# Loading q and k four heads per transfer, 18 tokens to a partition, in an attention and mixer kernel

## The chip, the cores and the metric

The kernel runs on one core of a Trainium2 chip. The metric is the device time of one execution in microseconds (us), as the median of several runs. The engines are PE (TensorE, the matrix unit), DVE (VectorE), ACT (ScalarE), POOL (GpSimd) and SP (SyncE, which here issues most of the DMA transfers). PEld is the loading of PE's weights. The granted clock is the share of PE's full clock that the chip's throttle allowed, as the profile reports it. In lines of the profile, L823 is a line of the kernel's source (the same line is L824 in the changed kernel), and names such as pmx or uTa are the kernel's buffers. A quad below is the set of four heads (of eight) that the kernel loads and processes together.

## The reference

The shapes are batch 8, heads 8, sequence 576, head dimension 64. Causal attention with a position bias from a running sum is followed by a token mixer and a channel mixer:

```python
def _attn_ref(q, k, v, s):
    scores = scale * np.matmul(q, k.transpose(0, 1, 3, 2))
    cum = np.cumsum(np.maximum(s, 0.0), axis=-1)
    bias = -(cum[:, :, :, None] - cum[:, :, None, :])
    scores = np.where(causal, -1000000000.0, scores + np.minimum(bias, 0.0))
    # ... softmax over the last axis, then attn @ v

def _moe_ref(x, w_tok1, w_tok2, w_ch1, w_ch2):
    h = np.maximum(x.transpose(0, 2, 1) @ w_tok1, 0.0) @ w_tok2
    u = x + h.transpose(0, 2, 1)
    h2 = np.maximum(u @ w_ch1, 0.0) @ w_ch2
    return u + h2
```

q and k are drawn with a standard deviation of 0.1, so that q·k/8 is of the order of 0.01. The bias dominates the scores.

## The kernel before

The kernel holds a planner in Python. It collects operations with an estimated cost for each engine that may run them, simulates the engines, and emits the instructions in the order that the simulation gave. An operation with several alternatives (for instance an eviction on ACT or DVE) goes where the simulation has room. The program keeps this order: every engine is given its own fixed list. Where PE has nothing to do in the plan's first 95 us, the planner also puts filler products of zeros; they are presumably meant to keep PE's clock up.

The parts that the change touches are the load of q and k, and the block transposes that consume it:

```python
    R = 2
    # ... ring of four fp32 buffers of [128, 1152], ring of four bf16 ones
    def load_quad(src, b, qd):
        f = Buf(r_qf)
        for g in range(4):
            load_op(lambda g=g: nc.sync.dma_start(
                out=f.t[32 * g : 32 * g + 32, :].rearrange("p (k n) -> p k n", n=R * D),
                in_=src[b, 4 * qd + g, :, :].rearrange("(k p r) d -> p k (r d)", p=32, r=R)),
                [(f, g)], S / R * 0.027 / 16)
        return f
    # ... the quad is cast to bf16 (on POOL, except for batch 0), then
            P.op(dve(576, lambda n=n, dst=dst: nc.vector.transpose(
                out=dst.t[:, 0:S, :].rearrange("d t e -> d (t e)").bitcast(FP32).rearrange(
                    "d (k p r) -> d k r p", p=32, r=R),
                in_=n.t[:, :].bitcast(FP32))), ...)
```

Each head takes 32 partitions. With R = 2, a partition holds nine runs of two neighbouring tokens (512 bytes each in DRAM). DVE transposes blocks of 32×32 four-byte elements (pairs of bf16); the 32 values that a block writes to one partition belong to tokens two apart, so they lie 8 bytes apart. `dve(576, ...)` is the planner's estimate for a transpose: 0.67 us.

## Time and profile before

332.36 us is the median of 3 runs (332.08 to 334.28). The profiled run's span is 333.4 us.

The page's busy line of the kernel before gives each engine's busy time, its share of the span and its instructions:

```profile
PE 300.1 (90%) x2557; PEld 167.4 (50%) x2593; DVE 181.4 (54%) x404; ACT 168.6 (51%) x269; POOL 86.8 (26%) x110
```

PE is busy nine tenths of the time, but the groups by line add 29.4 us of filler, and the chain of waits (the work that ended last, followed back to what released it, as shares of the span by engine and by line) says that a large part of the span was not set by PE:

```profile
PE 42%; DMA 29%; SPq 11%; DVE 9%; issue 4%; POOL 2%; ACT 1%; POOLq 0%; ACTq 0%; DVEq 0%
PE pmx L823 19%; PE pmx L841 15%; DMA qkf<-in_q_dram 12%; SPq L535 7%; DMA qkf<-in_k_dram 6%; SPq L562 4%; DMA wc<-in_moe_w_ch_dram 3%; DMA vf<-in_v_dram 3%; PE pmx L749 3%; DMA w<-in_moe_w_tok_dram 3%; PE pav L682 3%; DVE E L652 2%; PE psc L628 2%; POOL qkn L581 1%; DVE ub L777 1%
```

DMA, and SP's queue that issues it, hold 40% of the chain. In order of time they are most of its first 134 us; after that it is mostly PE. The table of stretches shows the same. Its columns are the stretch in us from the span's start, its length, busy us and instructions of each engine, the granted PE clock, the DMA engines' busy share (over 1 where packets overlap) and GB/s:

```profile
core 0: us, PE busy (x) PEld busy (x) DVE busy (x) ACT busy (x) POOL busy (x), PEclk, DMA share, GB/s
0.00:40.00 40.00, 33.42 (x277) 18.18 (x281) 25.38 (x64) 16.62 (x19) 16.81 (x39) 0.91 1.17 193
40.00:90.00 50.00, 43.93 (x472) 27.59 (x479) 30.71 (x69) 28.28 (x46) 24.83 (x24) 0.98 1.15 217
90.00:140.00 50.00, 42.98 (x366) 24.46 (x368) 29.79 (x68) 28.97 (x48) 18.57 (x19) 0.89 1.12 199
140.00:230.00 90.00, 84.22 (x729) 44.83 (x739) 55.83 (x118) 55.93 (x88) 26.59 (x29) 1.00 0.83 172
230.00:310.00 80.00, 78.65 (x636) 43.74 (x643) 36.20 (x84) 35.03 (x62) 0.00 (x0) 1.00 0.24 63
```

Up to 140 us the DMA share is above 1.1 at some 200 GB/s. In 90 to 140 us PE has 7.0 us of idle time and a clock of 0.89. Most of that idle time is one wait. In the list of PE's waits (who waited for whom: us in total, times, longest us) it comes first:

```profile
PE pmx L823 <- DMA uTa<-ua: 6.5, 1, 6.5
```

uTa is filled by transposing DMAs that SP issues in order, behind loads of q and k that are themselves waiting. One more line says how fast q and k come in. It is a stretch in which almost nothing but q and k moved:

```profile
124.00:128.00 4.00, 3.65 (x38) 1.58 (x36) 3.10 (x7) 1.94 (x2) 0.00 (x0) 1.00 1.24 203
```

203 GB/s is typical of such stretches. The packet records of the trace have 46,080 packets of 512 bytes for q and k, 45 ns long in the median and 27 ns at the tenth percentile.

The transposes, by their source line, with minimum, median and maximum in ns:

```profile
L607 DVE STREAM_TRANSPOSE kT<-qkn x16: 760/776/780, 9.5 to 242.7; 128x576 f32<-128x576 f32 x16
L607 DVE STREAM_TRANSPOSE qT<-qkn x16: 729/770/781, 12.6 to 245.2; 128x576 f32<-128x576 f32 x16
```

### The profile page before, as it was taken

How to read it: one execution, taken by the hardware profiler on the slowest of the kernel's cores; microseconds unless marked ns; L12 is line 12 of the kernel's file. 1: busy time of each engine (PE TensorE's matmuls, PEld its weight loads, DVE VectorE, ACT ScalarE, POOL GpSimd, SP SyncE). 2: the span in 40 equal slices, each digit the busy share in tenths (PEclk: the TensorE clock that was granted, in tenths of full speed). 3: DMA queues.
4: the chain of work that ended last, by engine and by line, in shares of the span. 5: the costliest groups of instructions: out<-in, count | busy, mean ns of one | idle time of the engine just before them, and what ended most of it. 6: DMA issues, size and time to landing. Idle time of an engine off the chain costs nothing.

```text
span 333.4 us, 6640 instructions
## 1 busy us (share of the span) xinstructions
PE 300.1 (90%) x2557; PEld 167.4 (50%) x2593; DVE 181.4 (54%) x404; ACT 168.6 (51%) x269; POOL 86.8 (26%) x110
## 2 busy tenths in 40 slices
PE   6798999879799993899899998997999999999992
PEld 2356685435566441444466443543575445446640
DVE  4685642588678753116874583958561744350030
ACT  1364581347769455364397445973474418306500
POOL 3175225473737422051216120270000000000000
PEclk9599999999789999699999999999999999999997
DMA  8999999999999999898798279992400430042031
GB/s 153 202 195 208 208 215 203 183 251 223 227 208 187 203 202 186 209 227 195 152 246 163 58 176 233 180 176 73 102 2 0 90 134 2 34 95 79 3 96 69
DMA packets 109640, 50.45 MB, mean 151 GB/s; under 512 B 55904, under 2 KB 104416, under 8 KB 109600
## 3 DMA queue, kind: packets, MB, share of 16 engines
q1 hardware_dynamic: 106192, 46.17, 70.3%
q0 software_dynamic: 3408, 3.77, 6.7%
q8 instruction: 22, 0.36, 0.5%
q14 instruction: 18, 0.15, 0.2%
HBM read 40.71 MB, written 9.44 MB: 150 GB/s over the span
## 4 chain that ended last, share of the span: by engine, by line
PE 42%; DMA 29%; SPq 11%; DVE 9%; issue 4%; POOL 2%; ACT 1%; POOLq 0%; ACTq 0%; DVEq 0%
PE pmx L823 19%; PE pmx L841 15%; DMA qkf<-in_q_dram 12%; SPq L535 7%; DMA qkf<-in_k_dram 6%; SPq L562 4%; DMA wc<-in_moe_w_ch_dram 3%; DMA vf<-in_v_dram 3%; PE pmx L749 3%; DMA w<-in_moe_w_tok_dram 3%; PE pav L682 3%; DVE E L652 2%; PE psc L628 2%; POOL qkn L581 1%; DVE ub L777 1%
## 5 line engine op out<-in xcount | busy, mean ns | idle before, releaser
L823 PEld LDWEIGHTS <-wc 128*128 128x128 bf16 x624 | 59.6, 100 | 41.9 <-issue 12.1
L647 ACT ACTIVATE E<-psc 128x1024 bf16<-128x1024 f32 x64 | 62.1, 1020 | 31.1 <-PE psc L628 30.4
L823 PE MATMUL pmx<-uTb,wc 128*128 128x320 bf16 x384 | 58.1, 306 | 0.3 <-DMA uTb<-us 0.2
L581 POOL CAST qkn<-qkf 128x1152 bf16<-128x1152 f32 x29 | 34.1, 1183 | 87.4 <-DMA qkf<-in_k_dram 23.9
L841 PE MATMUL pmx<-wc,gb 128*128 128x512 bf16 x231 | 54.3, 379 | 0.4
L823 PE MATMUL pmx<-uTa,wc 128*128 128x512 bf16 (+1 forms) x236 | 46.4, 345 | 7.7 <-DMA uTa<-ua 6.5
L830 ACT ACTIVATE gb<-pmx 128x320 bf16<-128x320 f32 x74 | 32.1, 438 | 35.4 <-PE pmx L823 31.0
L544 POOL TENSOR_TENSOR vp<-vf,wT 128x512 bf16<-128x512 f32 (+1 forms) x35 | 37.0, 1078 | 35.8 <-PE pav L682 21.1
L841 PE MATMUL pmx<-wc,ga 128*128 128x512 bf16 x184 | 44.3, 379 | 0.9 <-issue 0.3
L569 ACT ACTIVATE junk<-qkn 128x1152 bf16<-128x1152 bf16 x24 | 27.9, 1162 | 24.1 <-POOL qkn L581 23.7
L652 DVE TENSOR_TENSOR E<-E,keep 128x512 bf16<-128x512 bf16 x64 | 32.5, 514 | 13.6 <-ACT E L647 13.4
L841 PEld LDWEIGHTS <-gb 128*128 128x128 bf16 x240 | 22.5, 98 | 25.2 <-issue 0.4
L682 PEld LDWEIGHTS <-E 128*128 128x128 bf16 x576 | 26.4, 98 | 15.5 <-DVE E L660 2.5
L830 ACT ACTIVATE ga<-pmx 128x512 bf16<-128x512 f32 (+1 forms) x43 | 22.0, 515 | 21.8 <-PE pmx L823 18.0
L694 DVE TENSOR_TENSOR x<-pav,rc 128x320 bf16<-128x320 f32 x60 | 29.4, 491 | 1.8
L682 PE MATMUL pav<-vp,E 128*128 128x65 bf16 x540 | 27.4, 195 | 3.2 <-DVE E L660 2.1
L927 PE MATMUL pmx<-zero 128*128 128x512 bf16 (+5 forms) x88 | 26.4, 431 | 2.7 <-DVE zero L424 1.2
L689 DVE RECIPROCAL rc<-pav 128x5 f32<-128x5 f32 x60 | 11.4, 189 | 30.2 <-PE pav L682 29.8
L841 PEld LDWEIGHTS <-ga 128*128 128x128 bf16 x192 | 17.6, 98 | 19.7 <-issue 1.1
L628 PE MATMUL psc<-qT,kT 32*128 32x256 bf16 (+2 forms) x640 | 23.8, 253 | 3.9 <-ACT E L647 3.2
L628 PEld LDWEIGHTS <-kT 32*128 32x128 bf16 x640 | 15.8, 93 | 16.1 <-issue 14.9
L852 DVE TENSOR_TENSOR of<-pmx,ua 128x512 f32<-128x512 f32 x16 | 10.9, 683 | 20.8 <-PE pmx L841 11.3
(81 smaller groups left out, 240.2 us busy)
## 6 DMA issues: line engine op xcount, KB each, us to landing
qkf<-in_k_dram SPq DMA_DIRECT2D x80, 144.0 KB, 4.8
qkf<-in_q_dram SPq DMA_DIRECT2D x80, 144.0 KB, 5.4
vf<-in_v_dram SPq DMA_DIRECT2D x32, 256.0 KB, 5.8
out_dram<-of SPq DMA_DIRECT2D x32, 256.0 KB, 2.5
wc<-in_moe_w_ch_dram POOLq DMA_DIRECT2D x8, 384.0 KB, 11.3
vf<-in_v_dram SPq DMA_DIRECT2D x8, 128.0 KB, 5.0
out_dram<-of SPq DMA_DIRECT2D x8, 128.0 KB, 2.4
w<-in_moe_w_tok_dram POOLq DMA_DIRECT2D x2, 256.0 KB, 8.8
```

The costliest lines, as they stand in the source:

```text
L544: eng.tensor_tensor(out=vp.t[p0 : p0 + n, c, :, 0:D], in0=vf.t[p0 : p0 + n, c, :, :], in1=wT[p0 : p0 + n, cw, b * H : b * H + H].unsqueeze ...
L569: P.op({"ACT": (1.2, 1.6, lambda: nc.scalar.activation(out=junk[:, :], in_=src.t[:, :], func=AF.Square, accum_out=sq[:, col : col + 1]))}, ...
L581: nc.gpsimd.tensor_copy(out=n.t[:, :], in_=f.t[:, :])
L628: nc.tensor.matmul(out=pss[g // 2].t[:, g % 2, c0 : c0 + z - a], lhsT=kT.t[rows, j0 : j0 + 128, e], rhs=qT.t[rows, a:z, e], start=(e == 0) ...
L647: nc.scalar.activation(out=E.t[:, :, gi * 512 : gi * 512 + 512], in_=ps.t[:, :, :], func=AF.Exp, scale=0.125)
L652: nc.vector.tensor_tensor(out=o, in0=o, in1=keep[:, :].unsqueeze(1).unsqueeze(1).to_broadcast([128, 2, 2, 128]), op=ALU.mult)
L682: nc.tensor.matmul(out=o[:, ic, 0 : D + 1], lhsT=E.t[:, hh, d0 : d0 + 128], rhs=vp.t[:, jc, h + hh, 0 : D + 1], start=(jc == j_lo), stop=( ...
L694: nc.vector.tensor_tensor(out=x.t[:, :, (h + hh) * D : (h + hh + 1) * D], in0=o[:, :, 0:D], in1=rc.t[:, :].unsqueeze(2).to_broadcast([128, ...
L823: nc.tensor.matmul(out=pm.t[:, 0 : e - a], lhsT=wc1[:, m, cc * 128 : cc * 128 + 128], rhs=uT.t[:, m, a:e], start=(m == 0), stop=(m == NMC ...
L830: lambda cc=cc, pm=pm, a=a, e=e: nc.scalar.activation(out=g.t[:, cc, a:e], in_=pm.t[:, 0 : e - a], func=AF.Relu),
L841: nc.tensor.matmul(out=pm.t[:, :], lhsT=g.t[:, cc, c * 128 : c * 128 + 128], rhs=wc2[:, cc, :], start=(cc == 0), stop=(cc == NCC - 1))
L927: f.fn = lambda t=r.tiles[slots[0]], n=n: nc.tensor.matmul(out=t[:, 0:n], lhsT=zero[:, 0:128], rhs=zero[:, 0:n], start=True, stop=True)
```

## The change

The intent is to load a whole quad in one transfer over 128 partitions, with 18 consecutive tokens (4,608 contiguous bytes) per partition. The price is that DVE's transposes write every 18th token, which is a step of 72 bytes. The planner's model of loads is adapted. A rule about claimed buffers is added to the planner too.

```diff
-                if b.slot is None:
+                if b.slot is not None:
+                    t = max(t, b.since)
+                else:
 ...
+                    b.since = r.free[i]
 ...
-    R = 2
+    R = 18
 ...
-        for g in range(4):
-            load_op(lambda g=g: nc.sync.dma_start(
-                out=f.t[32 * g : 32 * g + 32, :].rearrange("p (k n) -> p k n", n=R * D),
-                in_=src[b, 4 * qd + g, :, :].rearrange("(k p r) d -> p k (r d)", p=32, r=R)),
-                [(f, g)], S / R * 0.027 / 16)
+        load_op(lambda: nc.sync.dma_start(
+            out=f.t[:, :], in_=src[b, 4 * qd : 4 * qd + 4, :, :].rearrange("g (p r) d -> (g p) (r d)", r=R)),
+            [(f, 0)], 128 * 0.19 / 16)
```

The remaining lines of the diff replace the four keys (f, 0) to (f, 3) by one.

More of the change, by code (lines that the diff above doesn't have):

```diff
@@ L589, in stage_qk @@
                 alts["ACT"] = (*c_act(1152), lambda cast=cast: cast(2))
-            castop[(b, qd, i)] = P.op(alts, reads=[(f, g) for g in range(4)], writes=[(n, 0)],
+            castop[(b, qd, i)] = P.op(alts, reads=[(f, 0)], writes=[(n, 0)],
                                       prio=b * 10 + 4 * qd if b else 0)
@@ L597, in stage_sq @@
             f = load_quad(src, b, qd)
-            square(f, [(f, g) for g in range(4)], (b * 2 + qd) * 2 + i)
+            square(f, [(f, 0)], (b * 2 + qd) * 2 + i)
     xbuf = {}
```

## The prediction

> **What bounds the kernel now.** The busy table puts PE at 300.1 of 333.4 us (90%). The groups by line give 29.4 us of that to filler products of zeros (L927): 270.7 us is needed PE work, about 63 us is filler or idle. The table of 10 us stretches shows where: 0–40 us holds 20.4 us of filler and 6.6 idle; 60–90 us 7.9 filler and 5.9 idle; 120–140 us 6.8 idle, almost all one 6.5 us wait of L823 for uTa (a transposing DMA in SP's queue, behind q and k loads); 200–230 us about 3.7 idle. The granted clock falls to 0.5 for 6.8 us twice after such gaps (0.78 in 90–100, 0.66 in 130–140). The chain of waits agrees: DMA and SP's queue up to 134 us, PE afterwards.
>
> In that first part the DMA engines are full (share 1.0–1.3) but move only about 200 GB/s: 202 where q and k load alone. Their 512-byte packets take 27 ns at best, 45 on average; the stores' 2048-byte packets take 85.
>
> **What the change does.**
> - Loads: 160 transfers to 32 partitions become 40 to 128, and 46,080 packets of 512 B become 5,120 of 4,608 B. The Trainium skill, "SBUF — State Buffer", Door 1, says DMA bandwidth depends on how many of 16 ports the partitions reach; 32 neighbouring partitions reach 8. The trace's 202 GB/s, about half of what 2048-byte packets imply (16 × 2048 / 85 ns = 385), agrees. Estimate from the packet times: 190 ns for 4,608 B, so 1.6 us for a 590 KB quad instead of 2.9: about 52 us less DMA time over 40 quads. v (256-byte packets) doesn't change.
> - SP's queue: 120 issues of 0.45 us fewer, about 54 us.
> - VectorE: each of 32 block transposes writes with a step of 72 bytes instead of 8. The same page says that fewer than two hits on a 16-byte line cost bandwidth. Now 0.77 us; I expect 0.8 to 1.3, so 1–17 us more of VectorE (181 us busy), mostly off the critical path.
> - Order: the planner's model changes, so the order moves a little; 93 filler products instead of 107 (about 3 us).
>
> **What of it is on the critical path.** Start: the second quad of batch 0 arrives about 5 us earlier and the weights follow; the channel stage, which began at 39 us, begins 5–7 us earlier. 60–90 us: v, q, k of batch 1 arrive during the channel stage of batch 0; 4–8 of the 14 us go. 120–140 us: 4–7 go. Clock: 1–3. Late part: 0–2. New waits and slower transposes: 2–4 back. Sum: about 19 us.
>
> **Prediction:** 313 us, range 301 to 326. Chances: faster by over 2% 0.86, within 2% 0.11, slower 0.03.
>
> **Right or wrong in the profile:** q/k stretches at 330 GB/s or more; 4,608-byte packets near 190 ns; a quad lands within 4 us; first L823 product before 34 us; no PE wait for uTa over 3 us; filler at most 26 us; L607 0.8–1.3 us; PE work outside filler about 271 us.
>
> **What would make it wrong:** L607 at 2 us or more, so that VectorE and the softmax chain hold PE; large packets limited to 200–250 GB/s after all; weights limited by their own queue; early loads only moving the waits to POOL's cast and the four qkf buffers; the new order putting another DMA transpose behind blocked loads.

## The result and the profile after

The changed kernel takes 323.09 us (median of 4 runs, 321.15 to 323.81), beside 332.61 us for the kernel before. The ratio is 0.9683 with a 95% interval of 0.9632 to 0.9735: faster. Ratios here are the mean time of one kernel's fast runs over the mean of the other's fast runs of the same rounds, so they are not quite the ratio of the quoted medians. The gain is 9.5 us, and about 19 were forecast.

The busy line after:

```profile
PE 297.7 (92%) x2579; PEld 164.3 (51%) x2579; DVE 199.4 (62%) x409; ACT 165.1 (51%) x263; POOL 88.2 (27%) x111
```

DVE has gained 18 us of work. The chain of waits after:

```profile
PE 65%; DVE 28%; issue 2%; ACT 2%; DMA 1%; SPq 0%; DVEq 0%
PE pmx L842 25%; PE pmx L824 23%; DVE kT L608 5%; PE pmx L750 5%; DVE E L653 4%; PE psc L629 4%; PE pav L683 4%; DVE qT L608 4%; DVE E L661 3%; DVE x L695 3%; PE pmx L771 2%; DVE ub L778 2%; PE pmx L928 2%; DVE ga L833 1%; DVE ua L778 1%
```

DMA has gone from 29% to 1% and SP's queue from 11% to nothing, as was intended. In their place stands DVE: 28% instead of 9%, of which the transposes (L608) are 9 points. The stretches after, with the columns as before:

```profile
0.00:40.00 40.00, 32.90 (x270) 17.64 (x271) 29.34 (x62) 14.95 (x18) 18.88 (x40) 0.91 1.04 225
40.00:90.00 50.00, 44.59 (x493) 27.77 (x491) 39.56 (x79) 31.42 (x51) 30.62 (x29) 1.00 0.95 274
90.00:140.00 50.00, 48.49 (x428) 26.77 (x426) 32.70 (x71) 31.76 (x52) 13.10 (x14) 1.00 0.67 181
140.00:230.00 90.00, 86.31 (x759) 45.98 (x758) 64.89 (x129) 51.62 (x81) 25.61 (x29) 1.00 0.55 151
230.00:310.00 80.00, 79.83 (x612) 43.76 (x610) 30.84 (x69) 35.39 (x65) 0.00 (x0) 1.00 0.20 52
```

In 90 to 140 us, PE's idle time has dropped from 7.0 to 1.5 us and the clock has recovered from 0.89 to 1.00. In 40 to 90 us PE gained only 0.7 us of busy time (1.9 without filler, which fell from 9.0 to 7.8 us there), while DVE went from 30.7 to 39.6 busy us out of 50. In 140 to 230 us DVE is busy for 64.9 us instead of 55.8. The first 40 us show hardly more PE work than before: without filler, which is 20.4 us before and 19.3 after, it is 13.6 us instead of 13.0.

A stretch of q and k alone after:

```profile
14.00:18.00 4.00, 4.00 (x53) 2.40 (x52) 4.00 (x11) 3.88 (x4) 2.62 (x4) 1.00 0.98 397
```

397 GB/s is almost twice the 203 of before. The 5,120 packets of 4,608 bytes take 178 ns in the median. PE's longest waits after:

```profile
PE pav L683 <- DVE E L661: 3.7, 4, 1.4
PE pav L683 <- DVE x L695: 2.2, 5, 0.5
PE psc L629 <- DVE qT L608: 2.0, 3, 1.1
```

The wait for uTa is gone. Summed over its list, PE waits for a named releaser 16.9 us instead of 23.6, but 15.1 of the 16.9 are now waits for DVE, instead of 7.1. The transposes after:

```profile
L608 DVE STREAM_TRANSPOSE kT<-qkn x16: 1235/1249/1260, 6.7 to 231.0; 128x576 f32<-128x576 f32 x16
L608 DVE STREAM_TRANSPOSE qT<-qkn x16: 1228/1246/1251, 10.5 to 233.8; 128x576 f32<-128x576 f32 x16
```

Each costs 0.48 us more, which is 15.3 us over 32.

A useful clock for the whole run is the start of the token stage of each batch (in batch 0, of its second half), read from the timeline of PE, in us:

| stage | before | after | gained so far |
|---|---|---|---|
| token stage, batch 0 | 32.7 | 31.7 | 1.1 |
| first product of the channel stage, batch 0 | 39.0 | 39.6 | -0.6 |
| token stage, batch 1 | 77.1 | 74.8 | 2.3 |
| token stage, batch 2 | 107.8 | 103.8 | 4.0 |
| token stage, batch 3 | 147.8 | 140.6 | 7.2 |
| token stage, batch 4 | 181.7 | 172.9 | 8.8 |
| token stage, batch 5 | 220.6 | 210.8 | 9.8 |
| end of the span | 333.4 | 322.0 | 11.4 |

The forecast put the gain mostly into the first 140 us. It came spread over the run, and nothing came from the start.

### The profile page after: what moved, and what is told of

It is laid out like the page before. It is cut to its first block, busy times and chain, and to the rows that moved or that the text cites. A ratio compares the mean times of both kernels' runs of the same rounds, so it can differ in the third digit from the quotient of the medians.

```text
span 322.0 us, 6476 instructions
## 1 busy us (share of the span) xinstructions
PE 297.7 (92%) x2579; PEld 164.3 (51%) x2579; DVE 199.4 (62%) x409; ACT 165.1 (51%) x263; POOL 88.2 (27%) x111
## 4 chain that ended last, share of the span: by engine, by line
PE 65%; DVE 28%; issue 2%; ACT 2%; DMA 1%; SPq 0%; DVEq 0%
PE pmx L842 25%; PE pmx L824 23%; DVE kT L608 5%; PE pmx L750 5%; DVE E L653 4%; PE psc L629 4%; PE pav L683 4%; DVE qT L608 4%; DVE E L661 3%; DVE x L695 3%; PE pmx L771 2%; DVE ub L778 2%; PE pmx L928 2%; DVE ga L833 1%; DVE ua L778 1%
## 5 line engine op out<-in xcount | busy, mean ns | idle before, releaser
L824 PEld LDWEIGHTS <-wc 128*128 128x128 bf16 x624 | 58.5, 98 | 34.5 <-issue 5.1
L582 POOL CAST qkn<-qkf 128x1152 bf16<-128x1152 f32 x30 | 35.6, 1203 | 81.7 <-ACT E L648 45.3
L824 PE MATMUL pmx<-uTb,wc 128*128 128x320 bf16 x384 | 56.3, 299 | 0.5 <-DVE gb L833 0.3
L824 PE MATMUL pmx<-uTa,wc 128*128 128x512 bf16 (+1 forms) x240 | 45.3, 337 | 1.2 <-DVE ga L833 1.2
L842 PE MATMUL pmx<-wc,ga 128*128 128x512 bf16 x192 | 45.9, 379 | 0.3
L653 DVE TENSOR_TENSOR E<-E,keep 128x512 bf16<-128x512 bf16 x64 | 32.7, 515 | 4.9 <-ACT E L648 4.7
L831 ACT ACTIVATE ga<-pmx 128x512 bf16<-128x512 f32 (+1 forms) x38 | 19.1, 502 | 22.7 <-PE pmx L824 22.1
L928 PE MATMUL pmx<-zero 128*128 128x512 bf16 (+3 forms) x82 | 23.8, 429 | 1.6 <-DVE zero L427 1.2
L629 PE MATMUL psc<-qT,kT 32*128 32x256 bf16 (+2 forms) x640 | 22.5, 250 | 2.0 <-DVE qT L608 2.0
L608 DVE STREAM_TRANSPOSE kT<-qkn 128x576 f32<-128x576 f32 x16 | 20.0, 1251 | 6.9 <-PE psc L629 5.9
L853 DVE TENSOR_TENSOR of<-pmx,us 128x512 f32<-128x512 f32 x4 | 2.8, 692 | 33.0 <-PE pmx L842 33.0
```

The lines of the kernel that those rows point to most:

```text
L582: nc.gpsimd.tensor_copy(out=n.t[:, :], in_=f.t[:, :])
L608: P.op(dve(576, lambda n=n, dst=dst: nc.vector.transpose(out=dst.t[:, 0:S, :].rearrange("d t e -> d (t e)").bitcast(FP32).rearrange("d (k ...
L629: nc.tensor.matmul(out=pss[g // 2].t[:, g % 2, c0 : c0 + z - a], lhsT=kT.t[rows, j0 : j0 + 128, e], rhs=qT.t[rows, a:z, e], start=(e == 0) ...
L653: nc.vector.tensor_tensor(out=o, in0=o, in1=keep[:, :].unsqueeze(1).unsqueeze(1).to_broadcast([128, 2, 2, 128]), op=ALU.mult)
L824: nc.tensor.matmul(out=pm.t[:, 0 : e - a], lhsT=wc1[:, m, cc * 128 : cc * 128 + 128], rhs=uT.t[:, m, a:e], start=(m == 0), stop=(m == NMC ...
L831: lambda cc=cc, pm=pm, a=a, e=e: nc.scalar.activation(out=g.t[:, cc, a:e], in_=pm.t[:, 0 : e - a], func=AF.Relu),
```

## The experiments

All of them are compared with the kernel before, run on the same chip. All passed the comparison with the reference. Where an edit makes the tokens of q and k come out in the wrong order, the comparison doesn't see it, for the reason given. All quoted medians are of fast runs, except for e5, a single look of unknown state, and e1, where one run of four is slow.

### e1: the large packets, but 32 partitions at a time

```diff
-        load_op(lambda: nc.sync.dma_start(out=f.t[:, :], in_=src[b, 4 * qd : 4 * qd + 4, ...]), ...)
+        def four():
+            for g in range(4):
+                nc.sync.dma_start(out=f.t[32 * g : 32 * g + 32, :],
+                                  in_=src[b, 4 * qd + g, :, :].rearrange("(p r) d -> p (r d)", r=R))
+        load_op(four, [(f, 0)], 128 * 0.19 / 16)
```

> The changed kernel with its order of instructions kept, but each quad of heads loaded by four transfers of 32 partitions, with the same 4608-byte packets. Ports theory (32 neighbouring partitions reach half of the ports): packets stretch from 178 ns to about 340 ns in the median, and stretches of q and k alone stay at 200 to 218 GB/s. Rival, packet size (the 512-byte packets were the limit): packets stay near 178 to 220 ns and stretches pass 300 GB/s. In time: with the ports theory most of the gain goes, 327 to 334 us; with the rival only the SP queue's extra issues count, 322 to 326 us. Result right.

The time was 328.45 us (ratio 0.9924, interval 0.9845 to 1.0002). One of the four runs, 332.98 us, is slow, and this ratio can only be reproduced with it counted in. The three fast runs have a median of 328.19 us, and without the slow run the ratio would be about 0.988. So more than half of the gain is gone either way, but the slow run must not be read as part of the effect. A stretch of q and k alone:

```profile
15.00:22.00 7.00, 6.79 (x88) 4.15 (x87) 6.21 (x17) 5.09 (x5) 4.30 (x6) 1.00 1.03 234
```

The packets took 291 ns in the median instead of 178. So packet size alone moves the rate from 203 to 234 GB/s, and one transfer over 128 partitions instead of four over 32 from 234 to 397. The DMA engines had packets all through this stretch (share 1.03), so a lack of issues is unlikely to have kept the rate down. The ports theory holds in kind. Its figure of 200 to 218 GB/s was too strict, and packet size has a share of its own. Small packets over 128 partitions were not run. The time also contains the extra issues on SP's queue, which this run doesn't separate.

### e2: the changed loads without the price on DVE

```diff
-                    "d (k p r) -> d k r p", p=32, r=R),
+                    "d (k p r) -> d k r p", p=32, r=2),
```

> The changed kernel, same order of instructions, but the 32 block transposes write every 2nd token again (step of 8 bytes) although the data are laid out for every 18th: the result is wrong on purpose, the work is that of the change without its cost on VectorE. Theory A (the transposes' extra 0.48 us each lie largely on the path, because VectorE is now in the chain of waits): transposes back at 0.77 us and 312 to 318 us. Theory B (they lie off the path; the gain was lost to other waits): transposes at 0.77 us and 320 to 323 us.

The time was 314.3 us (ratio 0.9491, interval 0.9418 to 0.9564), and the transposes were back at 0.77 us:

```profile
L608 DVE STREAM_TRANSPOSE kT<-qkn x16: 739/770/789, 6.6 to 221.7; 128x576 f32<-128x576 f32 x16
```

The order of instructions is that of the changed kernel. So the 15.3 us of extra DVE work cost 8.8 us of the 323.09: theory A. That is the difference of medians. By the ratios to the kernel before (0.9683 and 0.9491, one of e2's four runs being 318.35 us) it is 6.4 us. Without that price, the loads would have gained 18.2 us against the 332.52 of the kernel before in these rounds (16.9 by the ratio).

### e3: the price on DVE without the changed loads

```diff
-                    "d (k p r) -> d k r p", p=32, r=R),
+                    "d (k p r) -> d k r p", p=32, r=18),
```

This is the kernel before, with that one edit.

> The kernel before with only the write step of the transposes changed from 8 to 72 bytes, loads as before: wrong result on purpose. Transposes at 1.25 us if the step alone is the cause (0.77 if the arriving data were). Theory A: 3 to 9 us slower than before. Theory B: within 1.5 us of before.

The transposes took 1.24 to 1.25 us in the median, so the step alone is the cause:

```profile
L607 DVE STREAM_TRANSPOSE kT<-qkn x16: 1239/1253/1262, 9.3 to 243.1; 128x576 f32<-128x576 f32 x16
```

The time was 335.78 us (ratio 1.0092, interval 1.003 to 1.0154): 3.3 us slower, at the low end of theory A's range. The same extra work costs 8.8 us (6.4 by the ratios) where DMA no longer holds the run, and 3.3 us where it does. That fits the reading that removing one bound made the other engine's work dearer; the two kernels also have different orders of instructions, which these runs don't separate.

### e4: the planner told the truth

```diff
-            P.op(dve(576, lambda n=n, dst=dst: nc.vector.transpose(
+            P.op(dve(1135, lambda n=n, dst=dst: nc.vector.transpose(
```

`dve(1135)` means 1.25 us. The number is only the planner's estimate; the work is the same.

> The changed kernel with the planner told that a transpose takes 1.25 us on VectorE (it believed 0.67): the order of instructions and the share between VectorE and ScalarE change, nothing else. Theory A: 1 to 5 us faster than the changed kernel. Theory B: within 1.5 us of it. Result right.

The time was 314.32 us (ratio 0.9468, interval 0.9427 to 0.9509), with a right result. The transposes still took 1.25 us each, and DVE was still busy for 195.2 us (199.4 in the changed kernel), yet all of the 8.8 us came back (7.1 by the ratios), more than was expected. PE's waits for DVE fell from 15.1 us in 27 waits to 6.3 in 12; in e2 they are 10.1. The chain of waits of e4:

```profile
PE 71%; DVE 13%; ACT 6%; issue 4%; DMA 3%; POOL 0%; SPq 0%; DVEq 0%; ACTq 0%; POOLq 0%
PE pmx L842 25%; PE pmx L824 25%; PE pmx L928 5%; PE psc L629 5%; PE pmx L750 4%; PE pav L683 4%; ACT junk L570 3%; PE pmx L771 3%; ACT E L648 2%; DVE E L653 2%; DVE ub L778 2%; DVE E L661 2%; DVE kT L608 2%; DMA qkf<-in_q_dram 1%; DMA qkf<-in_k_dram 1%
```

DVE is at 13% instead of 28%, and PE at 71%. So the extra 0.48 us per transpose need not cost what e2 measured. By PE's waits, what cost the time was in the main an order of instructions made for transposes of 0.67 us: PE reached products whose operands came later than planned, and waited at the head of its list. That nothing of the cost is left in e4 is not shown. e4 also gives DVE 4.2 us less work, and e4 with the cheap step of 8 bytes, which would measure what the transposes still cost in its order, was not run.

### e5: what the step costs

```diff
-                    "d (k p r) -> d k r p", p=32, r=R),
+                    "d (k p r) -> d k r p", p=32, r=(1, 2, 3, 6, 9, 18, 1, 2)[b]),
```

> The changed kernel with a different write step of the transposes in each batch: 4, 8, 12, 24, 36, 72, 4 and 8 bytes for batches 0 to 7 (result wrong on purpose wherever it isn't 72). Theory of lines (a write that finds no second hit on its 16-byte line costs extra): 4 and 8 bytes at 0.77 us or a little less, 24, 36 and 72 all alike at 1.25 us, 12 bytes in between. Rival (cost grows with the distance): rising from 12 through 36 to 72 bytes.

The single time is 315.59 us. One transpose of kT from each of batches 0 to 5, that is at steps of 4, 8, 12, 24, 36 and 72 bytes, from the timeline of DVE (start, us, instruction):

```profile
18.59 0.77 DVE L608 STREAM_TRANSPOSE kT<-qkn 128x576 f32<-128x576 f32 x1
...
50.99 0.78 DVE L608 STREAM_TRANSPOSE kT<-qkn 128x576 f32<-128x576 f32 x1 [0.69 <-POOL qkn L582]
...
53.83 0.98 DVE L608 STREAM_TRANSPOSE kT<-qkn 128x576 f32<-128x576 f32 x1 [0.17 <-POOL qkn L582]
...
69.12 1.22 DVE L608 STREAM_TRANSPOSE kT<-qkn 128x576 f32<-128x576 f32 x1
...
103.51 1.21 DVE L608 STREAM_TRANSPOSE kT<-qkn 128x576 f32<-128x576 f32 x1
...
136.56 1.26 DVE L608 STREAM_TRANSPOSE kT<-qkn 128x576 f32<-128x576 f32 x1 [2.15 <-PE psc L629]
```

0.77 and 0.78 us at 4 and 8 bytes, 0.98 at 12, then 1.22, 1.21 and 1.26 at 24, 36 and 72. It is a step between 8 and 24 bytes, not a slope. The other transposes agree (0.73 to 0.78, 0.96 to 0.98, 1.20 to 1.26), and batches 6 and 7, back at 4 and 8 bytes, take 0.73 to 0.78 again, so it is not the place in the run. This is what the theory of lines says. R must divide 18, so the ladder has every choice, and none with more than two tokens per run avoids the price wholly.

### e6 and e7: was it the truth, or just another order?

e6 makes e4's edit in the kernel before, where it is false. e7 overstates the cost in the changed kernel:

```diff
-            P.op(dve(576, lambda n=n, dst=dst: nc.vector.transpose(
+            P.op(dve(1695, lambda n=n, dst=dst: nc.vector.transpose(
```

> Control for e4: the kernel before, whose transposes take 0.77 us, with its planner told 1.25 us. If e4 won because the planner learned the truth, this should gain nothing: within 1 per cent of before, or slower. If any reordering, or any bias against VectorE, gives such a gain by itself, this should be 2 per cent or more faster than before.

> Second control for e4: the changed kernel with its planner told 1.83 us for a transpose of 1.25. If the truth is what counts, it is slower than e4 (314 us) by 1 to 5 us, still faster than the changed kernel. If bias against VectorE is what counts, it is as fast as e4 or faster.

e6 took 334.46 us (ratio 1.0042, interval 0.9985 to 1.01): nothing gained. e7 took 318.8 us (ratio 0.959, interval 0.953 to 0.9649): better than 0.67, worse than 1.25. In the changed kernel the time as a function of what the planner believes is 323.1 at 0.67, 314.3 at 1.25 and 318.8 at 1.83. The true figure is the best of the three, and bias alone gives nothing in e6. Three points don't show how much the time moves with small changes of the figure, each of which makes a new order.

### e8: why the start moved so little

The data of the second quad arrived as forecast: its last cast ended at 17.9 us instead of 22.9. But DVE was still at earlier work and began the quad's transposes only at 20.0 us (before: 23.8), and they took longer, ending at 22.3 us instead of 25.2. Then the rest of the lead was lost in one instruction. The timeline of DVE in the changed kernel:

```profile
25.02 0.42 DVE L653 TENSOR_TENSOR E<-E,keep 128x512 bf16<-128x512 bf16 x1 [0.49 <-ACT E L648]
25.36 2.99 DVE L661 TENSOR_TENSOR E<-E,keep 128x128 bf16<-128x128 bf16 x1
28.27 0.41 DVE L653 TENSOR_TENSOR E<-E,keep 128x512 bf16<-128x512 bf16 x1
```

and that of POOL:

```profile
24.51 1.51 POOL L707 DMA_DIRECT2D wc<-in_moe_w_ch_dram  x2 [0.70 <-DMA w<-in_moe_w_tok_dram]
26.03 2.24 POOL L582 CAST qkn<-qkf 128x1152 bf16<-128x1152 f32 x2
```

The product with the mask in L661, normally 0.21 us, is recorded with 2.99 us and ends 0.08 us after POOL's two casts. The Trainium skill, "SBUF — State Buffer", section "SBUF: two separate sides", says that a DVE instruction with two SBUF inputs and a POOL instruction that reads SBUF share a pair of ports as an exclusive lock, and that whichever starts first holds it for its whole length. The common end agrees with such a lock. The order of starts does not: L661 is recorded 0.67 us before the first cast, in the time of POOL's DMA issues. Spans on POOL are rough, so this stays open. The experiment is e4 with these two casts moved to ACT, which had room (they ran there at 18.5 and 19.9 us):

```diff
+            if b == 1 and qd == 0:
+                alts = {"ACT": (*c_act(1152), lambda cast=cast: cast(2))}
             castop[(b, qd, i)] = P.op(alts, ...)
```

> e4 with the two casts of batch 1's first quad of heads moved from POOL to ScalarE. Theory: POOL's two casts hold back VectorE's products with the mask at 26 to 29 us (one of them took 2.99 us instead of 0.21 in the changed kernel), and this is why the channel stage started no earlier. Then those products are back under 0.6 us, the first product of the channel stage comes 1.5 to 3 us earlier than in e4, and the whole is 1 to 3 us faster than e4. Rival: the start is held by the transposes or the weights and nothing moves (within 1 us). Result right.

The time was 310.95 us (ratio 0.9323, interval 0.9279 to 0.9367), 3.4 us below e4, with a right result: the best kernel. The same products in e8's timeline of DVE:

```profile
26.22 0.42 DVE L655 TENSOR_TENSOR E<-E,keep 128x512 bf16<-128x512 bf16 x1 [0.28 <-ACT E L650]
26.56 0.22 DVE L663 TENSOR_TENSOR E<-E,keep 128x128 bf16<-128x128 bf16 x1
27.25 0.43 DVE L655 TENSOR_TENSOR E<-E,keep 128x512 bf16<-128x512 bf16 x1 [0.47 <-ACT E L650]
```

They are back at 0.22 and 0.43 us, and the first product of the channel stage came at 37.9 us instead of 41.6 in e4. So POOL's casts did lengthen the product. POOL's DMA issues alone did not: in e8 they are recorded from 21.03 to 26.32 us, and a product at 25.53 us took 0.41. Not all of the 3.4 us need be the hold. The casts also ran earlier, and the clock differs, as 30 to 40 us show in e4 and then in e8 (columns as before; the clock is the third figure from the end):

```profile
30.00:40.00 10.00, 8.10 (x76) 4.76 (x78) 8.04 (x18) 2.56 (x4) 0.36 (x2) 0.83 1.21 209
30.00:40.00 10.00, 9.32 (x88) 6.19 (x89) 6.89 (x17) 5.64 (x10) 0.54 (x2) 1.00 1.21 208
```

e4's profile has two drops of the clock to 0.5 before its end, of 3.4 us each; e8's has none (e2's has one). What such drops can be worth is seen within the changed kernel alone: its run with a mean clock of 0.994 took 321.15 us, the three with 0.983 to 0.985 took 322.83 to 323.81.

### e11: let the planner place more casts

This is e8, with `alts["ACT"]` added for all other casts of batches 1 to 7.

> e8, and for batches 1 to 7 the planner may give each remaining cast to POOL or ScalarE (it gives 8 more to ScalarE, 19 stay on POOL). If POOL's hold on VectorE costs time in the later stages too, 1 to 4 us faster than e8 (311 us); if it only mattered at the start, within 1.5 us of e8 or slower, because ScalarE takes 9 us more work. Result right.

The time was 312.74 us (ratio 0.9397, interval 0.9344 to 0.9449), slower than e8 by about 1.8 us, though on another chip and with overlapping intervals. POOL's work fell from 86.6 to 76.5 us and ACT's rose from 168.6 to 179.0. There is no sign that the hold costs anything further in later stages.

### e12: the casts moved, with the planner's old belief

This is the changed kernel with only e8's edit, run twice, the second time beside the changed kernel itself.

> The changed kernel (planner still believing 0.67 us for a transpose) with only the two casts of batch 1's first quad moved from POOL to ScalarE. Theory from e8 (the casts on POOL hold the start): the channel stage's first product comes before 38.5 us instead of 39.6, and the whole is 1 to 4 us faster than the changed kernel (323 us). Rival (what e8 gained needs the planner's new order): within 1 us of the changed kernel.

> The changed kernel again, on one chip with e12's repeat, to compare the two directly: ratio to before 0.966 to 0.971 as on record, about 323 us.

> e12 again, because its first result (0.9653, interval 0.9575 to 0.9731) could not be told from the changed kernel's 0.9683. If the lead that the moved casts give at the start lasts to the end, the ratio is 0.962 or lower, 2 us or more below after_again; if it is given back in later stages, within 1.5 us of after_again.

The first gave 322.02 us (ratio 0.9653, interval 0.9575 to 0.9731), not to be told from the changed kernel. The repeat gave 321.41 us (0.9647, interval 0.9604 to 0.969) beside 322.98 us for the changed kernel (0.9699, interval 0.9657 to 0.974). The channel stage started at 37.2 us in both profiles, 2.4 us earlier than in the changed kernel (2.0 earlier than in its repeat). Of that some 1.6 us is left at the end. The intervals of the ratios overlap, but all six runs of the repeat (318.31 to 322.07 us) lie below all six of the changed kernel beside it (322.29 to 323.83). The result falls between the two expectations. How much of e8's gain over e4 is the lock, how much the clock and how much the order around it stays open.

## Why the prediction was right, and where it was off

The direction and the range were right: 323.09 us lies between 301 and 326. The point of 313 us was 10 us too low, and the gain about half of the forecast's. The number was right because the range was 25 us wide: it covered a loss that the forecast had mis-sized. Point by point:

- **Loads: right.** 397 GB/s against "330 or more", and 178 ns per packet against 190. The reasoning from the ports holds with the correction of e1: packet size has a share. What the 120 issues fewer on SP's queue are worth by themselves, no run separates. "A quad lands within 4 us" was wrong: 5.4 to 5.8 us in the median from issue to landing, since a transfer may wait behind v's transfers in the same queue. What mattered was the queue's total.
- **The wait for uTa: right.** The 6.5 us wait is gone. From batch 2 to batch 3 the token stage gained 3.2 us, a little under the 4 to 7 that were forecast.
- **Clock: right in kind.** The two drops to 0.5 after gaps, 6.8 us each at about 88 and 132 us, are gone. The trace after has one drop of 3.4 us at 32 us in their place, besides the one at the start, which was halved.
- **What the loads are worth: about right in sum.** The forecast's gains add up to 14 to 27 us before the losses. e2, which has the changed loads and no dearer transposes, gains 18.2.
- **The transposes' size: right.** 1.25 us is inside 0.8 to 1.3, and 15.3 us more of DVE is inside 1 to 17.
- **"Mostly off the critical path", with 2 to 4 us back: wrong.** This is the step that failed. e2 puts the term at 8.8 us (6.4 by the ratios). The forecast argued from DVE's share of busy time (181 of 333 us). It did not ask what a static order does with an operation that takes nearly twice what the planner believes, although the prediction's own text says that the planner's model of the loads had changed and the diff leaves the cost of the transposes alone. e4 shows that correcting this mismatch wins back as much as the term; it does not show that the transposes cost nothing in its order.
- **Start 5 to 7 us earlier: wrong.** The data came 5.0 us earlier, but the channel stage started at 39.6 us instead of 39.0, where the forecast's own check was its first product before 34. DVE's list, the longer transposes and the hold by POOL's casts took it. Even the best runs started it only at 36.7 us (e2) and 37.2 us (e12).
- **60 to 90 us, 4 to 8 us less: mis-sized.** From the token stage of batch 0 to that of batch 1 the gain was 1.2 us. Without the dearer transposes (e2: batch 1 at 70.0 us, after 30.5 for batch 0) it is 4.8.
- **Filler at most 26 us: slightly off,** 27.1. Needed PE work, 297.7 - 27.1 = 270.6 us, is as forecast.

## What to carry to other kernels

When a DMA bound is lifted, look again at each engine whose work the change makes longer: the same 15 us of VectorE work cost 3.3 us under the old bound and 8.8 us (6.4 by the ratios) after it was gone. Where instructions are ordered by a model, correct the model in the same change; one number was worth 8.8 us here (7.1 by the ratios), nearly as much as the 9.5 us that the change had gained. And large packets are not enough: a load with 4,608-byte packets moved 234 GB/s in transfers of 32 partitions and 397 in one of 128.

## What the Trainium skill lacked or had wrong

- "SBUF — State Buffer", Specifications, says that fewer than two hits on a 16-byte line cost a penalty, but gives no size for writes of VectorE's block transpose. The runs show it for 128×576 four-byte elements: 0.77 to 0.78 us at steps of 4 and 8 bytes, 0.98 at 12, and 1.21 to 1.26 at 24, 36 and 72 (e5).
- "DMA: Bandwidth & Descriptors", Specifications, gives 512 bytes as the least transfer for line rate. On 32 partitions at a time, 512-byte packets moved 203 GB/s and 4,608-byte packets 234; on 128 partitions the latter moved 397. The part about ports on "SBUF — State Buffer" agrees with the larger of the two effects.
- "SBUF — State Buffer", section "SBUF: two separate sides", describes the lock between VectorE and GpSimd, but not how it looks in a profile: the hold that e8 removed appears as busy time of the VectorE instruction (2.99 us instead of 0.21), not as a wait.
